# Transpositions of the attention probabilities set between the matmuls of the expert block that follows, in a kernel of block attention and two mixture layers

## The chip, the cores and the metric

One core of a Trainium2 chip runs one program. The metric is device time in microseconds (us), the median of several executions; lower is better. The engines are PE (TensorE, matmuls; PEld is its loading of stationary operands), DVE (VectorE), ACT (ScalarE), POOL (GpSimd) and SP (SyncE, which issues the transfers). Each engine takes its own instructions strictly in the order in which they were recorded, and waits where one of them needs another engine's result.

## What is computed

Three stages follow one another: attention with a mask of 64-wide blocks (4 batches, 8 heads, 576 positions, head width 64), a layer that takes the largest of three products, and a gated layer.

```python
scores = np.where(block_i >= block_j, scale * np.matmul(q, k.transpose(0, 1, 3, 2)), -1e9)
attn = np.exp(scores - np.max(scores, axis=-1, keepdims=True))
attn = attn / (np.sum(attn, axis=-1, keepdims=True) + 1e-09)
x = np.matmul(attn, v)                      # 2304 tokens of 512
h = np.maximum(np.maximum(x @ w1, x @ w2), x @ w3)      # 768 wide
x = h @ w_out
gate = 1.0 / (1.0 + np.exp(-(x @ w_gate)))              # 1536 wide
out = gate * (x @ w_val) @ w_out2
```

## The kernel before

**Jobs.** A job is the attention of one batch and one pair of heads. The 16 early jobs take the first 256 positions, the 16 late jobs the other 320. A late job makes scores for head 0 and head 1 (`scores`, L390 and L391) and for the last 64 positions of both heads (`scores_four`, L460 and L461), takes maxima and exponentials on DVE and ACT, divides by the sums in place (tiles `E0`, `E1` and `E4`), transposes the probabilities on PE (`turn`, L493: 7 transpositions of 128x128 for each head in a late job, 3 in an early one; `turn_four`, L509: 4 and one of 64 columns), copies them out of PSUM into `PT` (`keep`, `keep_four`; lines L81 and L85 are the shared copy helper on ACT and DVE), and multiplies by the values (`apply`, L531). A late job's 7 transpositions fall into a group of 4 and a group of 3, each with a PSUM tile `ps_t` of its own. There are two such tiles, so a third group waits until the first has been copied out.

**Chunks.** The first layer runs in chunks 0 to 7 of 256 or 320 tokens: chunks 0 to 3 are the early halves (256 columns), 4 to 7 the late ones (320 columns). A chunk has 18 expert blocks, named here f0 to f5 with w0, w1 and w2 for the three weights (`experts`, L564 to L566), each of 12 matmuls that fill one tile `ps_m`, and four output blocks (`project`, L630 to L632) of 18. There are two `ps_m` tiles, so each block waits until the tile of the block before the last has been read. Reading it (`larger`) is ACT's copy for w0 and DVE's maximum (L603) for w1 and w2. After w2 the result is split into a high half on ACT (L614) and a low half on DVE (L90, tile `HR`), which the output blocks read. Chunk 0 uses another form (L584 and L592). The second layer (from 488 us) has no attention beside it.

**What runs beside what.** While chunk i runs, four jobs of the next chunk's attention run between its blocks: jobs of early halves in chunks 0 to 2, late jobs in chunks 3 to 6. PE takes both in one stream.

**What sets the order.** The kernel builds a list of operations (`Op`) with estimated costs, plans start times on all engines with them (`plan`), and records everything by planned start (`run_plan`). The chip then runs each engine's recorded order; the estimates set the order alone. `pe(...)` gives the cost of an operation on PE, `lat` and 0.25 us are added behind an operation of PE before its readers may start, and `LEN` spaces out the parts of the jobs. The planned cost of a group of transpositions is 0.109 us each and 0.02.

```python
kp = Op(*both(128 * len(g), True), lambda e, h=h, g=g: keep(j, h, g, e), [o] + pold)
o.frees = [kp]
```

These two lines say that the copy depends on its group of transpositions and that the group's `ps_t` tile is free when the copy is done; `both` lets the plan choose DVE or ACT.

Of the kernel before, what the change touches and what calls it, by code (L numbers as in the profile page):

```python
# [20 lines left out]
KD = DM // 128  # L21
# [12 lines left out]
QKN = 2 * S + 640  # L34

NEAR = 6


PLAN = {
# [27 lines left out]
def block_attention_moe_moe(ctx: ExitStack, tc, k1, q1, v1, k2, q2, vt, wa, wb, out):  # L67
# [3 lines left out]
    P = PLAN  # L71
# [65 lines left out]
    class Op:  # L137
# [3 lines left out]
        def __init__(self, eng, cost, f, deps, pos=None, ring=None, late=None, size=0):  # L141
            self.eng, self.cost, self.f = eng, cost, f
            self.deps = [d for d in deps if d is not None]
            self.pos, self.ring, self.late, self.size = pos, ring, late, size
            self.frees = []
            self.end = None
            self.late_pools = False
            ops.append(self)

    def act(n, acc=0):  # L150
# [8 lines left out]
    def plan():  # L159
# [60 lines left out]
        while left:  # L220
            picks = []
            for e in "PVAS":
                if e == "P":
                    c = choose([s[0] for s in pe if s], e)
                elif e in "VA":
                    c = choose(pools[e] + pools["B"], e)
                    if c is not None and c[1].eng == "B":

                        o, x = c[1], "VA"["AV".index(e)]
                        mine, other = o.cost["VA".index(e)], o.cost["VA".index(x)]  # L230
                        if max(free[x], c[2]) + other + 0.02 < c[2] + mine + (P["lean"] if e == "V" else 0.0):
                            c = choose(pools[e], e) if pools[e] else None
                else:
                    c = choose(pools[e], e)
                if c is not None:
                    picks.append((c[2], e, c[1]))
            assert picks, "the plan is stuck"
            t, e, o = min(picks, key=lambda x: (x[0], "SPVA".index(x[1])))
            cost = o.cost["VA".index(e)] if o.eng == "B" else o.cost
            if e == "P" and t < P["cold"]:  # L240
                cost *= 1.9
            o.start, o.on = t, e
            free[e] = t + cost
            o.end = t + cost
            if e == "S" and o.size:
                wire[0] = max(wire[0], t) + o.size / P["rate"]
                o.end = wire[0]
            if o.ring:
                rings[o.ring].append(o)
            if e == "P":  # L250
                pe["AM".index(o.stream)].pop(0)
            else:
                pools[o.eng].remove(o)
            for s in succ[o]:
                waiting[s] -= 1
                if waiting[s] == 0 and s.eng != "P":
                    pools[s.eng].append(s)
            left -= 1
# [12 lines left out]
    def run_plan():  # L271
        if SHOW:
            for o in sorted(ops, key=lambda o: o.start):
                if o.eng == "P":
                    print(f"{o.start:.2f} {o.end:.2f} {o.stream} {o.ring} pos {o.pos:.2f}")
            for e in "PVAS":
                print(e, sum(o.end - o.start for o in ops if o.on == e), max(o.end for o in ops if o.on == e))
            for w in range(0, 600, 25):
                print(w, [round(sum(max(0, min(o.end, w + 25) - max(o.start, w)) for o in ops if o.on == e), 1) for e in "PVA"])
        spare = []  # L280
        tensor = sorted([o for o in ops if o.eng == "P"], key=lambda o: o.start)
        end = 2.0
        for o in tensor:
            if o.ring == "m":
                break
            n = int((o.start - end) / P["turn"][bool(spare)])
            if n > 0:
                x = Op("P", 0.0, lambda n=n: keep_warm(n), [])
                x.start = end + 0.01
                spare.append(x)  # L290
            end = o.end
        for o in sorted(ops, key=lambda o: o.start):
            if o.late_pools and not WB:
                open_pools()
            at(o.start)
            o.f(o.on) if o.eng == "B" else o.f()

    warm = []

# [181 lines left out]
    def recip_four(j):  # L481
# [3 lines left out]
        )  # L485
        V.reciprocal(j.rc4, j.rc4)

    def turn(j, h, g):

        ps = ps_t.tile([128, 512], F32, tag="t", name="ps_t")  # L490
        for i, (k, t) in enumerate(g):
            e = EO[t] + j.eo + 128 * k
            T.transpose(ps[:, 128 * i : 128 * i + 128], E[h][:, e : e + 128], ident)  # L493
        j.tp[h, g[0]] = ps

    def keep(j, h, g, e):
# [8 lines left out]
    def turn_four(j, i):  # L505
        ps = ps_t.tile([128, 512], F32, tag="t", name="ps_t4")
        for k in ((0, 1, 2, 3), (4,))[i]:
            r = 64 if k == 4 else 128
            T.transpose(ps[0:r, 128 * (k % 4) : 128 * (k % 4) + 128], E4[:, 128 * k : 128 * k + r], ident)  # L509
        j.tp4[i] = ps.rearrange("p (k h c) -> p k h c", k=4, h=2)  # L510

    def keep_four(j, i, e):
# [44 lines left out]
    def experts(i, f, w):  # L557
        c = i // B
        n = CH1[c][1]
        xh, xl = xt(i, c, 0), xt(i, c, 1)  # L560
        ps = pm.tile([128, 512], F32, tag="m", name="ps_m")[:, :n]
        wt = W[f].rearrange("p s (w k c) -> p s w k c", w=3, k=KD)
        for k in range(KD):
            T.matmul(ps, wt[:, 0, w, k], xh[:, k], start=(k == 0), stop=False)  # L564
            T.matmul(ps, wt[:, 0, w, k], xl[:, k], start=False, stop=False)  # L565
            T.matmul(ps, wt[:, 1, w, k], xh[:, k], start=False, stop=(k == KD - 1))  # L566
        pss[i, f, w] = ps


# [50 lines left out]
    def project(i, d, fs):  # L620
        n = CH1[i // B][1]
        if 0 in fs:
            pss[i, d] = pm.tile([128, 512], F32, tag="m", name="ps_m")[:, :n]
        ps = pss[i, d]
        cd = slice(128 * d, 128 * d + 128)
        for f in fs:
            hh, hl = hcols(i, f)
            wo = W[6 + f // 3].rearrange("p s (f c) -> p s f c", f=3)
            wh, wl = wo[:, 0, f % 3, cd], wo[:, 1, f % 3, cd]
            T.matmul(ps, wh, hh, start=(f == 0), stop=False)  # L630
            T.matmul(ps, wh, hl, start=False, stop=False)
            T.matmul(ps, wl, hh, start=False, stop=(f == NF1 - 1))  # L632

    def stage(i, d, e):
        n = CH1[i // B][1]
# [47 lines left out]
    for j in jobs:  # L683
# [4 lines left out]
        else:  # L688
# [3 lines left out]
                v[0] = [(p, "T0"), (p, "T1")] + v[0]  # L692
            visits += v
    visits += [[], [(jobs[-1], "P")]]
    LEN = {"S0": (0, 0.82), "S1": (0.8, 0.82), "S4": (0, 1.06), "T0": (0.35, 0.77),
           "T1": (0.35, 0.77), "T4": (0, 0.5), "P": (0.95, 2.5)}
    place = {}
    ends = []
    for n, v in enumerate(visits):
# [36 lines left out]
    def build():  # L736
# [99 lines left out]
        def job(j):  # L836
# [94 lines left out]
            def turns(h):  # L931
                ns = [
                    Op(*both(128 * (t + 1), False), lambda e, h=h, k=k: norm(j, h, k, e), [rc[h]])
                    for k, t in enumerate(j.tiles)
                ]
                for q, g in enumerate(groups):
                    o = pe("A", 0.109 * len(g) + 0.02, lambda h=h, g=g: turn(j, h, g), ns, pos(f"T{h}") + 0.1 * q, ring="t")
                    kp = Op(*both(128 * len(g), True), lambda e, h=h, g=g: keep(j, h, g, e), [o] + pold)
                    kp.late = pos(f"T{h}") + P["keep"]
                    o.frees = [kp]  # L940
                    j.t_ops[h].append(o)
                    keeps.append(kp)

            def turns_four():
                for q in range(2):
                    o = pe("A", (0.45, 0.06)[q], lambda q=q: turn_four(j, q), [n4], pos("T4") + 0.1 * q, ring="t")
                    ks = [Op(*both((384, 128)[k], True), lambda e, k=k: keep_four(j, k, e), [o] + pold) for k in range(2)] if q == 0 else [
                        Op(*both(128, True), lambda e: keep_four(j, 2, e), [o] + pold)]
                    for k in ks:
                        k.late = pos("T4") + P["keep"]  # L950
                    o.frees = ks
                    j.t_ops[4].append(o)
                    keeps.extend(ks)
# [21 lines left out]
        def chunk(i):  # L975
# [5 lines left out]
            for f in range(NF1):  # L981
                m = []
                for w in range(3):
# [4 lines left out]
                        landed[3 * f + w].frees.append(o)  # L988
                    else:
                        o = pe("M", 12 * CM[c], lambda f=f, w=w: experts(i, f, w), deps, pos, ring="m")  # L990
                    if i == 2 * B - 1:
                        users[f].append(o)
                    if w == 0:
# [18 lines left out]
            for d in range(KD):  # L1012
# [16 lines left out]
                if i == 2 * B - 1:  # L1029
                    users[6].extend(done)  # L1030
                    users[7].extend(done)
                st = Op(*both(n, True), lambda e, d=d: stage(i, d, e), done, ring="st")
                st.late = pos + mcost(i, NF1) + P["evac"]
                o.frees = [st]
# [215 lines left out]
```

## Time and profile before

| | us |
|---|---|
| median of 3 runs (944.55 to 945.87) | 945.73 |
| profiled execution, its own time | 944.49 |
| its span, first to last instruction | 942.7 |
| PE busy | 934.0 (99%) |
| PEld busy | 865.3 (92%) |
| DVE busy | 475.2 (50%) |
| ACT busy | 379.6 (40%) |
| POOL busy | 0.7 |

Matmuls are pipelined: a row's duration is the way of one matmul through the engine, and what a matmul takes from its successors is the distance between their starts. Behind a group of transpositions the first matmul is recorded as started early and lasts longer; the start of the second matmul behind is free of that. PE's granted clock is 1.00 of full speed (the 2.4 GHz level) from 36 us on.

### The profile page before, as it was taken

The numbers are of one execution on the slowest core, as the hardware profiler recorded it, in microseconds if no ns is written. First come the engines' busy times: TensorE is split into PE (matmuls) and PEld (weight loads), VectorE is DVE, ScalarE is ACT, GpSimd is POOL, SyncE is SP. The second block draws the span as 40 slices with busy tenths as digits, with TensorE's granted clock in tenths as the row PEclk, the third lists the DMA queues.
The fourth block names the chain that finished last, engine by engine and source line by source line (L and its number), as shares of the span: only waits on it lengthen the run. The fifth ranks groups of instructions, "written<-read, shape, count | busy, mean of one in ns | idle before, by whom it ended". The sixth has DMA issues, their size and how long they took to land.

```text
span 942.7 us, 14791 instructions
## 1 busy us (share of the span) xinstructions
PE 934.0 (99%) x5891; PEld 865.3 (92%) x5891; DVE 475.2 (50%) x1215; ACT 379.6 (40%) x901; POOL 0.7 (0%) x6
## 2 busy tenths in 40 slices
PE   7999999999999999999999999999999999999998
PEld 6888999999999999999999999999999999999997
DVE  5998546786776776765359961122113112112111
ACT  5946433565654655653247742112112112111111
POOL 0000000000000000000000000000000000000000
PEclk9999999999999999999999999999999999999999
DMA  8921123222122323102047750001000000000000
GB/s 296 363 62 57 35 86 99 64 93 78 54 77 82 121 79 104 40 1 69 27 159 258 263 182 34 1 3 48 1 1 34 1 1 34 1 0 1 34 1 34
DMA packets 38437, 70.16 MB, mean 74 GB/s; under 512 B 5856, under 2 KB 23264, under 8 KB 38368
## 3 DMA queue, kind: packets, MB, share of 16 engines
q1 hardware_dynamic: 38368, 69.22, 22.1%
q8 instruction: 46, 0.75, 0.3%
q14 instruction: 23, 0.19, 0.1%
HBM read 59.77 MB, written 9.44 MB: 73 GB/s over the span
## 4 chain that ended last, share of the span: by engine, by line
PE 98%; SPq 1%; DMA 0%; DVE 0%; issue 0%; ACT 0%
PE ps_m L564 7%; PE ps_m L565 7%; PE ps_m L566 7%; PE ps_g L1145 5%; PE ps_g L1143 5%; PE ps_out L1174 5%; PE ps_out L1175 5%; PE ps_g L1144 5%; PE ps_v L1145 5%; PE ps_v L1143 5%; PE ps_v L1144 5%; PE ps_out L1173 5%; PE ps_o L531 5%; PE ps_t L493 4%; PE ps_m L584 3%; PE ps_m L630 3%
## 5 line engine op out<-in xcount | busy, mean ns | idle before, releaser
L1153 DVE TENSOR_TENSOR gv<-ps_v,sg 128x384 f32<-128x384 f32 x72 | 40.1, 557 | 269.2 <-PE ps_v L1145 253.1
L564 PE MATMUL ps_m<-XT,w 128*128 128x320 f32 (+1 forms) x504 | 155.1, 308 | 0.0
L566 PE MATMUL ps_m<-XT,w 128*128 128x320 f32 (+1 forms) x504 | 150.2, 298 | 0.0
L565 PE MATMUL ps_m<-XT,w 128*128 128x320 f32 (+1 forms) x504 | 150.1, 298 | 0.0
L1149 ACT ACTIVATE sg<-ps_g 128x384 f32<-128x384 f32 x72 | 35.4, 491 | 178.0 <-PE ps_g L1145 178.0
L564 PEld LDWEIGHTS ps_m<-XT,w 128*128 128x128 f32 x504 | 95.4, 189 | 3.4 <-issue 1.9
L565 PEld LDWEIGHTS ps_m<-XT,w 128*128 128x128 f32 x504 | 95.5, 190 | 0.7
L566 PEld LDWEIGHTS ps_m<-XT,w 128*128 128x128 f32 x504 | 95.3, 189 | 0.0
L1160 ACT CAST HR<-gv 128x384 fp32r<-128x384 f32 x72 | 36.9, 512 | 129.1 <-DVE gv L1153 128.9
L439 ACT ACTIVATE E<-ps_s,nm 128x384 f32<-128x384 f32 (+1 forms) x124 | 64.6, 528 | 54.1 <-DVE nm L434 34.5
L603 DVE TENSOR_TENSOR m<-ps_m,m 128x320 f32<-128x320 f32 (+1 forms) x90 | 41.3, 459 | 55.6 <-PE ps_m L566 52.7
L1145 PE MATMUL ps_g<-XT,w 128*128 128x384 f32 x192 | 64.8, 338 | 0.0
L1143 PE MATMUL ps_g<-XT,w 128*128 128x384 f32 x192 | 64.7, 337 | 0.0
L1143 PE MATMUL ps_v<-XT,w 128*128 128x384 f32 x192 | 64.2, 334 | 0.0
L1145 PE MATMUL ps_v<-XT,w 128*128 128x384 f32 x192 | 64.2, 334 | 0.0
L1175 PE MATMUL ps_out<-w,HR 128*128 128x512 f32 x144 | 57.0, 396 | 0.0
L1174 PE MATMUL ps_out<-w,HR 128*128 128x512 f32 x144 | 56.9, 395 | 0.0
L1173 PE MATMUL ps_out<-w,HR 128*128 128x512 f32 x144 | 56.0, 389 | 0.0
L90 DVE TENSOR_TENSOR HR<-gv,HR 128x384 fp32r<-128x384 f32 x72 | 40.2, 558 | 30.6 <-ACT HR L1160 30.6
L434 DVE TENSOR_REDUCE nm<-ps_s 128x1 f32<-128x384 f32 (+1 forms) x124 | 54.0, 470 | 0.8
L531 PE MATMUL ps_o<-PT,v 128*64 128x320 f32 (+3 forms) x448 | 50.5, 365 | 3.3 <-DVE PT L85 3.3
L630 PE MATMUL ps_m<-HR,w 128*128 128x320 f32 (+1 forms) x168 | 51.8, 308 | 0.0
(136 smaller groups left out, 2071.6 us busy)
## 6 DMA issues: line engine op xcount, KB each, us to landing
wraw<-in_wb_dram SPq DMA_DIRECT2D x36, 512.0 KB, 4.5
wland<-in_wa_dram SPq DMA_DIRECT2D x6, 1536.0 KB, 16.7
qk<-in_k_dram SPq DMA_DIRECT2D x16, 576.0 KB, 4.0
v<-in_vt_dram SPq DMA_DIRECT2D x16, 320.0 KB, 2.9
xraw<-x2d SPq DMA_DIRECT2D x12, 384.0 KB, 3.6
out_dram<-osb SPq DMA_DIRECT2D x18, 256.0 KB, 2.1
wraw<-in_wa_dram SPq DMA_DIRECT2D x6, 512.0 KB, 5.7
qk<-in_q_dram SPq DMA_DIRECT2D x16, 160.0 KB, 4.3
```

The source lines that it names most:

```text
L439: A.activation(E[h][:, e : e + 128 * (t + 1)], j.s[h, t], AF.Exp, bias=j.nm[:, c : c + 1], scale=1.0 if j.late else SCALE, accum_out=j.sm[ ...
L531: T.matmul(j.o[rows(h), d : d + n], j.v[:, h, k, :], PT[:, h, c : c + n], start=(k == 0), stop=(k == len(parts) - 1), skip_group_check=True,)
L564: T.matmul(ps, wt[:, 0, w, k], xh[:, k], start=(k == 0), stop=False)
L565: T.matmul(ps, wt[:, 0, w, k], xl[:, k], start=False, stop=False)
L566: T.matmul(ps, wt[:, 1, w, k], xh[:, k], start=False, stop=(k == KD - 1))
L630: T.matmul(ps, wh, hh, start=(f == 0), stop=False)
L1143: T.matmul(ps, w[:, 0, i, k], xh[:, k], start=(k == 0), stop=False)
L1144: T.matmul(ps, w[:, 0, i, k], xl[:, k], start=False, stop=False)
L1145: T.matmul(ps, w[:, 1, i, k], xh[:, k], start=False, stop=(k == KD - 1))
L1173: T.matmul(ps, gh[:, ct], wh, start=(f == 0), stop=False)
L1174: T.matmul(ps, gh[:, ct], wl, start=False, stop=False)
L1175: T.matmul(ps, gl[:, ct], wh, start=False, stop=(f == NF2 - 1))
```

## The change

The transpositions are no longer recorded where their operation stands. `turn` and `turn_four` put them on a list, and the next operation of PE decides: if it is an expert or output block of chunks 1 to 7, `matmul` records the listed transpositions one by one among that block's matmuls, evenly; if it is anything else, or if a copy that reads them is recorded first, they are recorded at once, in a row, as before.

The estimates change too. In late jobs and all but the first few early ones (`i > 3`) a transposition now costs 0.068 us in the plan instead of 0.109, a group counts as done 0.25 us times its number of transpositions later (`lag`), and `LEN` is shorter for the three parts with transpositions.

```diff
+TC = (0.109, 0.068)
+TLAG = 0.25
...
+            self.lag, self.blends = 0.0, False
...
-            o.end = t + cost
+            o.end = t + cost + o.lag
...
+        due = []
         for o in sorted(ops, key=lambda o: o.start):
...
+            if due and (o.eng == "P" and not (o.blends or o.lag) or any(d in due for d in o.deps)):
+                turn_some(len(turns_due))
+                due = []
+            if o.lag:
+                due.append(o)
             at(o.start)
             o.f(o.on) if o.eng == "B" else o.f()
+            if o.eng == "P" and not o.lag:
+                turn_some(len(turns_due))
+                due = []
...
+    def turn_some(n):
+        for _ in range(n):
+            o, x = turns_due.pop(0)
+            T.transpose(o, x, ident)
+
+    def among(n):
+
+        shares[:] = [0, n, len(turns_due)]
+
+    def matmul(*a, **k):
+        i, n, m = shares
+        if turns_due:
+            turn_some(-((-(i + 1) * m) // n) - (m - len(turns_due)))
+        shares[0] += 1
+        T.matmul(*a, **k)
...
-            T.transpose(ps[:, 128 * i : 128 * i + 128], E[h][:, e : e + 128], ident)
+            turns_due.append((ps[:, 128 * i : 128 * i + 128], E[h][:, e : e + 128]))
...
+        among(3 * KD)
...
-            T.matmul(ps, wt[:, 0, w, k], xh[:, k], start=(k == 0), stop=False)
+            matmul(ps, wt[:, 0, w, k], xh[:, k], start=(k == 0), stop=False)
...
-    LEN = {"S0": (0, 0.82), "S1": (0.8, 0.82), "S4": (0, 1.06), "T0": (0.35, 0.77),
-           "T1": (0.35, 0.77), "T4": (0, 0.5), "P": (0.95, 2.5)}
+    LEN = {"S0": (0, 0.82), "S1": (0.8, 0.82), "S4": (0, 1.06), "T0": (0.35, 0.5),
+           "T1": (0.35, 0.5), "T4": (0, 0.36), "P": (0.95, 2.5)}
...
-                    o = pe("A", 0.109 * len(g) + 0.02, lambda h=h, g=g: turn(j, h, g), ns, pos(f"T{h}") + 0.1 * q, ring="t")
+                    o = pe("A", TC[i > 3] * len(g) + 0.02, lambda h=h, g=g: turn(j, h, g), ns, pos(f"T{h}") + 0.1 * q, ring="t")
+                    if i > 3:
+                        o.lag = TLAG * len(g)
...
-                    o = pe("A", (0.45, 0.06)[q], lambda q=q: turn_four(j, q), [n4], pos("T4") + 0.1 * q, ring="t")
+                    o = pe("A", (4, 1)[q] * TC[1] + 0.02, lambda q=q: turn_four(j, q), [n4], pos("T4") + 0.1 * q, ring="t")
+                    o.lag = TLAG * (4, 1)[q]
```

The place shown below is the second job of chunk 5 (about 324 to 332 us in the trace of before). On PE before, its 7 transpositions of `E0` stand in a row between block f2 w0 (`ps_m_3955`) and block f2 w1 (`ps_m_3987`):

```order
L566 MATMUL ps_m_3955<-XT_76,w_848 128x320
L493 MATMUL ps_t_3977<-ident_101,E0_107 128x128 x4
L493 MATMUL ps_t_3983<-ident_101,E0_107 128x128 x3
L564 MATMUL ps_m_3987<-XT_76,w_848 128x320
L565 MATMUL ps_m_3987<-XT_76,w_848 128x320
```

On PE now, from the third transposition of `E0` in that job on; the block around them, `ps_m_3990`, is f2 w2, `ps_m_4017` is f3 w0 and `ps_m_4045` is f3 w1:

```order
L512 MATMUL ps_t_3985<-ident_101,E0_107 128x128
L523 MATMUL ps_m_3990<-XT_76,w_847 128x320 x2
L512 MATMUL ps_t_3985<-ident_101,E0_107 128x128
L523 MATMUL ps_m_3990<-XT_76,w_847 128x320
L512 MATMUL ps_t_3987<-ident_101,E0_107 128x128
L523 MATMUL ps_m_3990<-XT_76,w_847 128x320 x2
L512 MATMUL ps_t_3987<-ident_101,E0_107 128x128
L523 MATMUL ps_m_3990<-XT_76,w_847 128x320 x2
L512 MATMUL ps_t_3987<-ident_101,E0_107 128x128
L523 MATMUL ps_m_3990<-XT_76,w_847 128x320 x2
L523 MATMUL ps_m_4017<-XT_76,w_909 128x320 x12
L512 MATMUL ps_t4_4032<-ident_101,E4_109 128x128
```

The last transposition of `E0` now stands behind ten of the block's twelve matmuls, and the row of seven became seven rows of one.

On DVE before, the same job: the two copies of `E0`'s transpositions, the low half `L` of the next job's keys, two small operations on the sums, the maximum that reads `ps_m_3987`, and what follows:

```order
L377 SCALAR_TENSOR_TENSOR Q1_104<-qk_3810,Q1_104 64x320 x2
L85 COPY PT_110<-ps_t_3977 128x4x128
L85 COPY PT_110<-ps_t_3983 128x3x128
L90 TENSOR_TENSOR L_106<-qk_3582,K_105 128x1152
L447 TENSOR_SCALAR rc_3885<-sm_3884 128x2
L448 RECIPROCAL rc_3885<-rc_3885 128x2
L603 TENSOR_TENSOR m1_4032<-ps_m_3987,m0_4003 128x320
L87 TENSOR_SCALAR E1_108<-E1_108,rc_3885 128x384
L85 COPY PT_110<-ps_t4_4006 128x2x64
L85 COPY PT_110<-ps_t4_4011 64x2x64
L603 TENSOR_TENSOR m2_4043<-ps_m_4013,m1_4032 128x320
```

On DVE now, the same job:

```order
L89 COPY PT_110<-ps_t_3987 128x3x128
L89 COPY PT_110<-ps_t_3985 128x4x128
L94 TENSOR_TENSOR L_106<-qk_3571,K_105 128x1152
L463 TENSOR_SCALAR rc_3899<-sm_3898 128x2
L464 RECIPROCAL rc_3899<-rc_3899 128x2
L641 TENSOR_TENSOR m2_4041<-ps_m_3990,m1_3954 128x320
L91 TENSOR_SCALAR E1_108<-E1_108,rc_3899 128x384
L89 COPY PT_110<-ps_t4_4038 64x2x64
L393 SCALAR_TENSOR_TENSOR Q1_104<-qk_3811,Q1_104 64x320 x2
L89 COPY PT_110<-ps_t4_4032 128x2x64
L94 TENSOR_TENSOR HR_1025<-m2_4041,HR_1025 128x320
L641 TENSOR_TENSOR m1_4072<-ps_m_4045,m0_4039 128x320
```

The copy of the later group (`ps_t_3987`, three transpositions) moved ahead of that of the earlier one, the maximum behind the chain is now that of the block that holds the transpositions (`ps_m_3990`), and the products for `Q1` moved between the two copies of `E4`'s transpositions.

## Rows read from the trace of the kernel before

**Rows 1.** The page: span, PE's busy time, and the chain that ended last.

```profile
span 942.7 us, 14791 instructions
PE 934.0 (99%) x5891; PEld 865.3 (92%) x5891; DVE 475.2 (50%) x1215; ACT 379.6 (40%) x901; POOL 0.7 (0%) x6
PE 98%; SPq 1%; DMA 0%; DVE 0%; issue 0%; ACT 0%
```

**Rows 2.** All waits of PE: who waited for whom, us, times, longest.

```profile
PE ps_o L531 <- DVE PT L85: 3.3, 1, 3.3
PE ps_w L306 <- POOL ident masks.py:199: 1.4, 1, 1.4
PE ps_s L411 <- DMA qkv<-in_q_dram: 0.4, 1, 0.4
```

**Rows 3.** Timeline of PE: start, us, line; one transposition alone among matmuls of 256.

```profile
207.96 0.28 PE L565 MATMUL ps_m<-XT,w 128*128 128x256 f32 x1
208.08 0.28 PE L566 MATMUL ps_m<-XT,w 128*128 128x256 f32 x1
208.20 0.27 PE L509 MATMUL ps_t<-ident,E 128*64 128x128 f32 x1
208.23 0.36 PE L564 MATMUL ps_m<-XT,w 128*128 128x256 f32 x1
208.43 0.28 PE L565 MATMUL ps_m<-XT,w 128*128 128x256 f32 x1
```

**Rows 4.** Timeline of PE: seven transpositions in a row among matmuls of 320.

```profile
346.52 0.31 PE L565 MATMUL ps_m<-XT,w 128*128 128x320 f32 x1
346.67 0.31 PE L566 MATMUL ps_m<-XT,w 128*128 128x320 f32 x1
346.82 0.93 PE L493 MATMUL ps_t<-ident,E 128*128 128x128 f32 x7
347.50 0.40 PE L564 MATMUL ps_m<-XT,w 128*128 128x320 f32 x1
347.73 0.30 PE L565 MATMUL ps_m<-XT,w 128*128 128x320 f32 x1
```

**Rows 5.** Timeline of DVE, second job of chunk 5: start, us, line, idle before.

```profile
324.58 1.08 DVE L434 TENSOR_REDUCE nm<-ps_s 128x1 f32<-128x384 f32 x2
325.69 0.89 DVE L377 SCALAR_TENSOR_TENSOR Q<-qk,Q 64x320 fp32r<-64x320 f32 x2
326.67 1.16 DVE L85 COPY PT<-ps_t 128x512 f32<-128x512 f32 x2
327.74 1.35 DVE L90 TENSOR_TENSOR L<-qk,K 128x1152 fp32r<-128x1152 f32 x1
329.00 0.16 DVE L447 TENSOR_SCALAR rc<-sm 128x2 f32<-128x2 f32 x1
329.20 0.17 DVE L448 RECIPROCAL rc<-rc 128x2 f32<-128x2 f32 x1
329.29 0.49 DVE L603 TENSOR_TENSOR m<-ps_m,m 128x320 f32<-128x320 f32 x1
329.69 0.41 DVE L87 TENSOR_SCALAR E<-E,rc 128x384 f32<-128x384 f32 x1
330.02 0.47 DVE L85 COPY PT<-ps_t 128x128 f32<-128x128 f32 x2
331.82 0.56 DVE L85 COPY PT<-ps_t 128x384 f32<-128x384 f32 x1 [0.27 <-PE ps_t L493]
```

**Rows 6.** Timeline of PE, the same job: its transpositions and the next block.

```profile
326.03 0.93 PE L493 MATMUL ps_t<-ident,E 128*128 128x128 f32 x7
330.86 0.93 PE L493 MATMUL ps_t<-ident,E 128*128 128x128 f32 x7
331.54 0.40 PE L564 MATMUL ps_m<-XT,w 128*128 128x320 f32 x1
```

**Rows 7.** Groups by line (busy us, mean ns, idle before): low halves of h, DVE.

```profile
L90 DVE TENSOR_TENSOR HR<-m,HR 128x320 fp32r<-128x320 f32 (+1 forms) x42 | 19.2, 458 | 8.0 <-ACT HR L614 7.6
```

**Rows 8.** Busy us by engine in two stretches: chunks 1 to 3, chunks 4 to 6.

```profile
core 0: us, PE busy (x) PEld busy (x) DVE busy (x) ACT busy (x) POOL busy (x), PEclk, DMA share, GB/s
84.00:236.00 152.00, 152.00 (x1246) 140.68 (x1245) 100.83 (x299) 73.15 (x208) 0.00 (x0) 1.00 0.24 73
236.00:437.00 201.00, 201.00 (x1444) 187.46 (x1443) 141.36 (x378) 116.61 (x283) 0.00 (x0) 1.00 0.21 66
```

More of the change, by code (lines that the diff above doesn't have):

```diff
@@ L486, in recip_four @@
         V.reciprocal(j.rc4, j.rc4)
+    turns_due = []
+    shares = [0, 0, 0]
+    def turn_some(n):
[10 more added lines that the diff above has]
+        T.matmul(*a, **k)
     def turn(j, h, g):
@@ L508, in turn_four @@
             r = 64 if k == 4 else 128
-            T.transpose(ps[0:r, 128 * (k % 4) : 128 * (k % 4) + 128], E4[:, 128 * k : 128 * k + r], ident)
+            turns_due.append((ps[0:r, 128 * (k % 4) : 128 * (k % 4) + 128], E4[:, 128 * k : 128 * k + r]))
         j.tp4[i] = ps.rearrange("p (k h c) -> p k h c", k=4, h=2)
@@ L562, in experts @@
         wt = W[f].rearrange("p s (w k c) -> p s w k c", w=3, k=KD)
+        among(3 * KD)
         for k in range(KD):
-            T.matmul(ps, wt[:, 0, w, k], xh[:, k], start=(k == 0), stop=False)
-            T.matmul(ps, wt[:, 0, w, k], xl[:, k], start=False, stop=False)
-            T.matmul(ps, wt[:, 1, w, k], xh[:, k], start=False, stop=(k == KD - 1))
+            matmul(ps, wt[:, 0, w, k], xh[:, k], start=(k == 0), stop=False)
+            matmul(ps, wt[:, 0, w, k], xl[:, k], start=False, stop=False)
+            matmul(ps, wt[:, 1, w, k], xh[:, k], start=False, stop=(k == KD - 1))
         pss[i, f, w] = ps
@@ L625, in project @@
         cd = slice(128 * d, 128 * d + 128)
+        among(3 * len(fs))
         for f in fs:
@@ L629, in project @@
             wh, wl = wo[:, 0, f % 3, cd], wo[:, 1, f % 3, cd]
-            T.matmul(ps, wh, hh, start=(f == 0), stop=False)
-            T.matmul(ps, wh, hl, start=False, stop=False)
-            T.matmul(ps, wl, hh, start=False, stop=(f == NF1 - 1))
+            matmul(ps, wh, hh, start=(f == 0), stop=False)
+            matmul(ps, wh, hl, start=False, stop=False)
+            matmul(ps, wl, hh, start=False, stop=(f == NF1 - 1))
     def stage(i, d, e):
@@ L990, in chunk @@
                         o = pe("M", 12 * CM[c], lambda f=f, w=w: experts(i, f, w), deps, pos, ring="m")
+                        o.blends = True
                     if i == 2 * B - 1:
@@ L1031, in chunk @@
                     users[7].extend(done)
+                for o1 in done:
+                    o1.blends = i > 0
                 st = Op(*both(n, True), lambda e, d=d: stage(i, d, e), done, ring="st")
```

## The prediction

> **What bounds the kernel now.** I read the chain that ended last first: 98% of the span is PE [rows 1]. Then PE's waits: three in the whole run, 5.1 us together, all in the first 19 us [rows 2]. From chunk 1 on PE is busy in every stretch (152.00 of 152, 201.00 of 201 us), with DVE at 66% and 70% and a granted clock of 1.00 [rows 8]. So from chunk 1 on the time is the sum of what PE's instructions take from one another. A change can gain only by making one of them cheaper, and every wait that it puts on PE is paid in full. Two questions decide: what a transposition costs between two matmuls, and whether the copies behind the transpositions still come in time.
>
> **What a spread transposition costs.** Seven in a row: from the first start to the start of the second matmul behind them 347.73 - 346.82 = 0.91 us, less that matmul's predecessor's own 0.147 (346.67 to 346.82) leaves 0.763, or 0.109 each [rows 4]. The trace of before also holds the form that the change makes: one transposition alone between two expert blocks. There 208.43 - 208.20 = 0.23, less the 0.12 that a matmul of 256 columns takes (207.96 to 208.08), leaves 0.11 [rows 3]. So alone costs as much as in a row. That row loads 64 columns of probabilities where most have 128, but it streams the same 128 columns and a load is under way while the matmul ahead runs; a larger load gives no reason for a lower price. The change spreads 234 of the 400 transpositions (222 alone, 6 pairs); the rest are in chunk 0's time, or, like the 7 of `E1` in 15 of 16 late jobs, still stand in a row, since what follows them there is no expert block. At 0.11 against 0.109 the spreading is worth 0 to -0.3 us. Lower bound of the price: half of a 256-column matmul, 0.06, which would give 234 x 0.049 = 11.5 us back. I take 0.11, since the row is the thing itself.
>
> The Trainium skill, "TensorE: Matmul & The Clock Gate", speaks for that lower bound: section "Back-to-back issue gap" gives 128 / 2.4 + 2.5 = 56 ns for 128 columns, and "Weight-path perf modes" says that a load of 128 columns of a type other than FP32 is fast, so the matmul behind would not be held up. By it the gain would be an estimated 234 x 0.053 = 12.4 us. The single row at 0.11 disagrees.
>
> **What the copies cost now.** The planned lag is 1.0 us behind a group of four and 0.75 behind a group of three, so the plan expects the later group of three first and puts its copy first. On the chip the transpositions are spread through the whole block, and the last comes late. I set 0 at the first transposition of `E0` and walk the second job of chunk 5. The last one starts behind ten matmuls and six transpositions: 10 x 0.147 + 6 x 0.109 = 2.12. It ends 0.27 later, and a copy starts 0.03 behind the end of its group (330.86 + 0.93 = 331.79, copy at 331.82 [rows 5, 6]): 2.42. DVE, which takes its instructions in order, stands at that copy. Its reductions of the scores run as in before from 0.4 to 1.5, so it is free by then. Behind the two copies stand the low half of the keys, the two small operations and the maximum that frees the block's `ps_m`; the same chain in before took 329.29 + 0.49 - 326.67 = 3.11 [rows 5]. So `ps_m` comes free at 5.53. PE reaches the block that needs it (f3 w1, two blocks on) at 12 x 0.147 + 7 x 0.109 = 2.53, plus 1.76 for f3 w0, plus 0.11 for one transposition of `E4`: 4.40. With 0.05 for the hop, an estimate from the 0.03 above, PE waits **1.2 us**. In before the chain began at 326.67 and its `ps_m` was wanted at 331.54 behind the `E1` row [rows 6], 1.76 us after 329.78: covered. That cover is gone.
>
> The same job waits again. PE resumes at 5.58; nine matmuls and three transpositions on, the last of `E4` starts at 7.23 and ends at 7.50. DVE copies it at 7.53, then takes the two `Q1` products (0.89) and then the second copy (the two copies 0.47 [rows 5]): 8.89. The seven transpositions of `E1` need that `ps_t`; PE is there after three matmuls, at 7.23 + 0.11 + 0.44 = 7.78: **1.15 us**. Chunks 4 and 6 have the same order in this job.
>
> Fourth job of chunks 4 to 6: copies (1.07 to the next start) and maximum (0.40) from 2.42, then the low half of the keys (1.26) and only then the low half of h of f5 (0.46 [rows 7]): 5.61. The output block's second matmul on f5 wants it at 2.53 + 15 x 0.147 + 4 x 0.109 + 0.147 = 5.32: **0.35 us**. First and third job: the maximum is ahead of the long operation, or ACT reads the block; no wait by the same walk. Sum for a chunk 2.7, for three **8.1 us**.
>
> Chunk 3 has 256 columns (0.12 each), and its last transposition is copied at 10 x 0.12 + 0.65 + 0.30 = 2.15. Second job: chain to the reciprocal's end 2.62, then a copy of `E4`'s last transposition (0.23) and a normalisation (0.33) ahead of the maximum (0.42): 5.75 against 2.20 + 1.44 + 5 x 0.11 = 4.19, **1.6**. Third job: DVE stands at the copy of `E4`'s last transposition, which starts at 3.64 + 9 x 0.12 + 4 x 0.109 = 5.16 and ends at 5.43, then 0.23 + 0.33 + 0.42 to the `ps_m` that f5 w0 wants at 5.63: 6.44, **0.85**. Fourth: low half of h at 5.25 against 4.67, **0.6**. Together **3.05 us**. Chunks 1 and 2 have early jobs, whose copies are followed by short operations, and two blocks or more of cover; 0.
>
> **The rest.** PE records the same instructions in the same number; DVE takes 27 more and ACT 27 fewer, some 0.5 us each of copies and scalings, over 353 us in which DVE is busy 242 [rows 8]: no bound of its own, but part of why both copies stand on DVE. The stage from 488 us is untouched in order. The last job's `E1` is spread three matmuls ahead of `apply`: 0 to 0.3.
>
> **The sum.** 8.1 + 3.05 + 0.2 = 11.3 us, against the profiled execution's own 944.49 (span 942.7 and 1.8 around it): 955.8. The median of the three runs lies 1.2 above that execution: 945.73 + 11.3 = **957.0**. Thirteen waits make the sum. If each link is 0.4 us quicker than in the walk, 11.3 - 5 gives 952; if each is 0.4 slower, 962.
>
> **The rivals.** *The transposition is cheap among matmuls.* For it: the columns themselves, 0.06. Against it: the single row, and the first transposition of each row, whose load was covered by a matmul and which still takes 0.109. Alone it gives 945.7 - 11.5 = 934; together with the waits 945.7 - 11.5 + 11.3 = 945.5, no change. *The copies hold nobody up* (not slower): PE gives DVE time elsewhere, or the copy of three does not stand at the last transposition, because its group ended sooner. The place is DVE's chain behind that copy, the price 1.2 us a job, and the point is a chain that ends before 4.40; it would have to be 1.1 us shorter than the 3.11 measured. Then the time is 945.7 to 946. For it: no wait at all in before, so the plan leaves room. Against it: the room of that chain was 1.76 and the block's spreading takes 1.36 of transposition time (2.12 - 0.76) on top of an order in which the wanted tile is one block earlier. *The change doesn't spread*: 166 of 400 are unspread, the others are in the recorded order, so this is out.
>
> **Chances.** Waits of 6 to 16 us: 0.72 (951.5 to 962). Smaller waits, 2 to 6 us: 0.06. Above 962: 0.04. Hardly any wait: 0.11. Cheap with waits: 0.04; cheap without: 0.03. About 0.2% (1.9 us) is what a measurement of this kernel can tell from no change, so faster 0.04, same 0.14, slower 0.82. The range holds the likeliest case and reaches down to the case without waits: 946 to 962.
>
> **What would show it.** Right: PE's waits on DVE's maximum (`m`) and on `PT` appear in the second job of chunks 3 to 6, 1 us or more each, and on `HR` in the fourth; the single transpositions are 0.11 apart from their matmul; DVE stands idle ahead of the copy of the group of three until the last transposition's end, about 2.4 us behind the first one. Wrong: the matmul behind a spread transposition starts 0.06 to 0.07 after it, or chunks 4 to 6 end as early as before.

## The result

954.81 us (median; 953.65 to 955.26) against 945.80 for the kernel before in the same runs: a ratio of 1.0091, 95% interval 1.0076 to 1.0106. The change makes the kernel 9.0 us slower. The prediction was 957.0, with a range of 946.0 to 962.0 and 0.82 on slower.

The page of the changed kernel: span, and busy time of each engine with the number of instructions (compare [rows 1]).

```profile
span 952.9 us, 14788 instructions
PE 939.0 (99%) x5891; PEld 864.8 (91%) x5891; DVE 484.5 (51%) x1242; ACT 366.5 (38%) x874; POOL 0.7 (0%) x6
```

PE's instructions are as many as before, DVE has 27 more and ACT 27 fewer. The waits of PE tell more. In before it had none after 19 us [rows 2]; now, from 84 to 500 us (who waited for whom, us in total, times, longest us):

```profile
PE ps_t L512 <- DVE PT L89: 1.8, 3, 0.6
PE ps_m L523 <- ACT m L639: 1.2, 3, 0.4
PE ps_m L523 <- DVE HR L94: 1.2, 4, 0.5
PE ps_m L523 <- DVE m L641: 0.7, 1, 0.7
```

Eleven waits, 4.9 us. A wait also costs what lies around it (matmuls that were in flight count as busy, and PE starts again slowly), so the whole price is better read from the lengths of the chunks: from the start of a chunk's first matmul to that of the next chunk's. The first matmul of chunk 5 starts at 305.73 in before, that of chunk 6 at 376.61; now it is 311.26 and 384.36:

```profile
305.73 0.31 PE L564 MATMUL ps_m<-XT,w 128*128 128x320 f32 x1
...
376.61 0.31 PE L564 MATMUL ps_m<-XT,w 128*128 128x320 f32 x1
```

```profile
311.26 0.46 PE L523 MATMUL ps_m<-XT,w 128*128 128x320 f32 x2
...
384.36 0.46 PE L523 MATMUL ps_m<-XT,w 128*128 128x320 f32 x2
```

So 70.88 us became 73.10. Worked out in the same way for every chunk (chunk 7 up to the first matmul of the second layer), from starts in ns:

| chunk | before, us | changed kernel, difference |
|---|---|---|
| 1 | 45.41 | -0.03 |
| 2 | 45.03 | -0.01 |
| 3 | 63.02 | +2.31 |
| 4 | 70.88 | +2.22 |
| 5 | 70.88 | +2.22 |
| 6 | 69.01 | +2.22 |
| 7 | 42.24 | 0.00 |

Together +8.9, which is the whole of the 9.0. The start of chunk 1 moves by up to 2.4 us from one profiled execution to another (81.4 in before, 82.4 here, 83.8 in one of the experiments) and is taken for noise: the executions of the kernel before alone lie from 943.79 to 947.46 us beside the first experiments. The chunks repeat to a few hundredths, and the experiments are read from them.

**Where the three losses of a chunk lie.** Chunk 5's second job on PE (start, us, engine, line, operation, shape, count, and in brackets the idle time ahead and what ended it), with the first and the last transposition of `E0` at its head:

```profile
333.32 0.27 PE L512 MATMUL ps_t<-ident,E 128*128 128x128 f32 x1
...
335.46 0.27 PE L512 MATMUL ps_t<-ident,E 128*128 128x128 f32 x1
335.49 2.29 PE L523 MATMUL ps_m<-XT,w 128*128 128x320 f32 x14
337.62 0.27 PE L512 MATMUL ps_t<-ident,E 128*128 128x128 f32 x1
338.29 0.56 PE L523 MATMUL ps_m<-XT,w 128*128 128x320 f32 x2 [0.41 <-ACT m L639]
...
340.70 0.66 PE L512 MATMUL ps_t<-ident,E 128*128 128x128 f32 x4
341.94 0.55 PE L512 MATMUL ps_t<-ident,E 128*128 128x128 f32 x3 [0.59 <-DVE PT L89]
```

The first loss is ahead of block f3 w1: a matmul behind a transposition is recorded 0.03 after it, here 0.68 after it. That is 0.65 later, and with the slower restart (0.25 to the next start instead of 0.23) about 0.68 in all. The second is in the row of `E1`, whose starts should be 0.109 apart: the fifth comes 1.24 after the first instead of 0.44; with 0.10 ahead of the first and 0.06 behind the fifth that is 0.96. The third is in the fourth job, at the output block:

```profile
370.28 0.38 PE L512 MATMUL ps_t<-ident,E 128*128 128x128 f32 x2
370.89 0.41 PE L523 MATMUL ps_m<-HR,w 128*128 128x320 f32 x1 [0.23 <-DVE HR L94]
```

0.61 from the pair's start where 0.11 and 0.03 are usual: 0.47, and with the slower restart about 0.5. 0.68 + 0.96 + 0.50 = 2.14 of the 2.22.

DVE in the second job, the rows that answer to [rows 5]:

```profile
333.63 1.08 DVE L450 TENSOR_REDUCE nm<-ps_s 128x1 f32<-128x384 f32 x2
335.77 1.15 DVE L89 COPY PT<-ps_t 128x384 f32<-128x384 f32 x2 [1.06 <-PE ps_t L512]
336.84 1.35 DVE L94 TENSOR_TENSOR L<-qk,K 128x1152 fp32r<-128x1152 f32 x1
338.11 0.16 DVE L463 TENSOR_SCALAR rc<-sm 128x2 f32<-128x2 f32 x1
338.30 0.17 DVE L464 RECIPROCAL rc<-rc 128x2 f32<-128x2 f32 x1
338.38 0.47 DVE L641 TENSOR_TENSOR m<-ps_m,m 128x320 f32<-128x320 f32 x1
338.77 0.41 DVE L91 TENSOR_SCALAR E<-E,rc 128x384 f32<-128x384 f32 x1
340.36 0.28 DVE L89 COPY PT<-ps_t 64x128 f32<-64x128 f32 x1 [1.19 <-PE ps_t L512]
340.68 0.89 DVE L393 SCALAR_TENSOR_TENSOR Q<-qk,Q 64x320 fp32r<-64x320 f32 x2
341.60 0.29 DVE L89 COPY PT<-ps_t 128x128 f32<-128x128 f32 x1
```

It is done with the reductions at 334.71 and stands idle for 1.06 at the copy of the group of three, as forecast; they start 335.77 - 333.32 = 2.45 us behind the first transposition (2.42 forecast). Then L, reciprocal and the maximum, to 338.85. From 84 to 437 us DVE's waits for a `ps_t` ahead of a copy grew from 6.9 to 24.8 us. In before the transpositions have two lines, L493 for `E0` and `E1` and L509 for `E4`; now all have one. The rows of before and of now:

```profile
DVE PT L85 <- PE ps_t L493: 6.7, 15, 0.9
DVE PT L85 <- PE ps_t L509: 0.2, 1, 0.2
```

```profile
DVE PT L89 <- PE ps_t L512: 24.8, 30, 1.2
```

One thing in these rows is not as forecast. The maximum that should have freed the tile for f3 w1 starts at 338.38, and PE goes on at 338.29, ahead of it. What ended its wait is ACT's copy of f3 w0, of the block that had only just ended; it ends at 338.24, 0.05 ahead of PE's start:

```profile
337.82 0.43 ACT L639 COPY m<-ps_m 128x320 f32<-128x320 f32 x1 [1.54 <-PE ps_m L523]
```

### The profile page after: what moved, and what is told of

It is laid out like the page before. It is cut to its first block, busy times and chain, and to the rows that moved or that the text cites. A ratio compares the mean times of both kernels' runs of the same rounds, so it can differ in the third digit from the quotient of the medians.

```text
span 952.9 us, 14788 instructions
## 1 busy us (share of the span) xinstructions
PE 939.0 (99%) x5891; PEld 864.8 (91%) x5891; DVE 484.5 (51%) x1242; ACT 366.5 (38%) x874; POOL 0.7 (0%) x6
## 4 chain that ended last, share of the span: by engine, by line
PE 96%; DVE 2%; SPq 1%; DMA 1%; issue 0%; ACT 0%
PE ps_m L523 28%; PE ps_g L1190 5%; PE ps_g L1188 5%; PE ps_out L1219 5%; PE ps_g L1189 5%; PE ps_out L1220 5%; PE ps_v L1190 5%; PE ps_v L1188 5%; PE ps_v L1189 5%; PE ps_out L1218 5%; PE ps_o L568 5%; PE ps_t L512 4%; PE ps_m L622 3%; PE ps_s L406 2%; PE ps_s L407 1%; PE ps_s L427 1%
## 5 line engine op out<-in xcount | busy, mean ns | idle before, releaser
L523 PE MATMUL ps_m<-XT,w 128*128 128x320 f32 (+1 forms) x1512 | 236.3, 310 | 1.9 <-ACT m L639 1.2
L523 PEld LDWEIGHTS ps_m<-XT,w 128*128 128x128 f32 x1512 | 212.6, 189 | 8.3 <-ACT m L639 2.2
L512 PE MATMUL ps_t<-ident,E 128*128 128x128 f32 (+1 forms) x400 | 86.3, 275 | 1.8 <-DVE PT L89 1.8
L523 PE MATMUL ps_m<-HR,w 128*128 128x320 f32 (+1 forms) x504 | 75.4, 303 | 1.2 <-DVE HR L94 1.2
L523 PEld LDWEIGHTS ps_m<-HR,w 128*128 128x128 f32 x504 | 69.7, 189 | 3.2 <-DVE HR L94 2.1
L89 DVE COPY PT<-ps_t 128x384 f32<-128x384 f32 (+3 forms) x89 | 45.9, 531 | 31.1 <-PE ps_t L512 29.4
L512 PEld LDWEIGHTS ps_t<-ident,E 128*128 128x128 f32 (+1 forms) x400 | 51.7, 140 | 4.7 <-DVE PT L89 3.3
```

What stands on the lines that cost most here:

```text
L89: n.tensor_copy(out, in_)
L512: T.transpose(o, x, ident)
L523: T.matmul(*a, **k)
```

## The experiments

Differences are those of chunks 3 to 6 against the kernel before, from starts of matmuls as above; chunks 1, 2 and 7 stay within 0.05 us in all of them.

| run | chunk 3 | 4 | 5 | 6 | median, us | ratio, 95% interval |
|---|---|---|---|---|---|---|
| changed kernel | 2.31 | 2.22 | 2.22 | 2.22 | 954.81 | 1.0091 (1.0076 to 1.0106) |
| row_in_new_plan | 0.23 | 0.23 | 0.23 | 0.23 | 947.05 | 1.0010 (1.0000 to 1.0020) |
| spread_over_6 | 0.83 | 1.01 | 1.02 | 1.04 | 950.31 | 1.0043 (1.0026 to 1.0060) |
| spread_over_9 | 1.41 | 1.77 | 1.76 | 1.75 | 952.28 | 1.0065 (1.0045 to 1.0085) |
| four_first | 1.50 | 1.73 | 1.73 | 1.69 | 953.32 | 1.0071 (1.0052 to 1.0089) |
| tiles_alternate | 3.35 | 2.80 | 2.81 | 2.84 | 956.57 | 1.0113 (1.0098 to 1.0128) |
| row_tiles_alternate | 1.35 | 0.00 | 0.00 | 0.00 | 947.01 | 1.0013 (1.0003 to 1.0022) |
| three_on_ACT | 1.69 | -0.45 | 2.44 | -0.74 | 948.86 | 1.0025 (1.0015 to 1.0036) |
| late_lag_alternate | 2.23 | 1.57 | 1.55 | 1.59 | 953.32 | 1.0078 (1.0061 to 1.0095) |
| e4_copy_on_ACT | 2.33 | 1.37 | 1.38 | 1.38 | 951.86 | 1.0060 (1.0043 to 1.0077) |

### In a row, in the new plan

```diff
             turns_due.append((ps[:, 128 * i : 128 * i + 128], E[h][:, e : e + 128]))
+        turn_some(len(turns_due))
         j.tp[h, g[0]] = ps
```

(and the same line in `turn_four`.)

> The changed kernel with its plan (costs, lags, the order of every engine) as it is, but each group of transpositions recorded at once, in a row, where its operation stands. Theory A (the waits come from the last transposition coming 2.4 us after the first, with DVE's in-order copies behind it): the seven end 0.93 us after the first, 1.5 us earlier than when spread; the waits of the second job of chunks 4 to 6 (0.68 and 0.95) and of the fourth (0.5) are gone, and those of chunk 3; time 945.8 to 947, chunks 3 to 6 within 0.5 us of the kernel before. Theory B (the waits come from the plan's new order: group of three first, Q1 between the copies of E4, 27 more operations on DVE, however early the transpositions come): they stay, 952 to 955. Theory C (a transposition among matmuls costs more or less than one in a row): the time of the row moves by 234 x the difference; at the 0.108 read from the changed kernel's trace that is nothing.

947.05, and 0.23 a chunk is left of 2.2. The second and the third loss of the result are gone, and of the first 0.23 is left; the order on DVE is the changed kernel's own. So what costs is how late the last transposition comes, and not the new order alone. Where that 0.23 comes from is shown below.

### Spread over nine and over six matmuls

The edit for six; for nine it has 9 in the place of 6.

```diff
-            turn_some(-((-(i + 1) * m) // n) - (m - len(turns_due)))
+            turn_some(min(m, -((-(i + 1) * m) // 6)) - (m - len(turns_due)))
```

> The changed kernel with the transpositions spread over the first nine of a block's matmuls instead of all twelve. Theory A: the last of E0's seven stands behind 7 matmuls instead of 10, 0.44 us earlier, so the first wait of the second job falls from 0.68 to about 0.25; the last of E4's five behind 7 instead of 9, 0.29 earlier, so the second falls from 0.95 to about 0.65; the fourth job's 0.5 to about 0.1. Per chunk 1.0 instead of 2.2, chunk 3 about 1.2 instead of 2.3; time about 950 (949 to 951.5). Theory B: 954 to 955, unchanged.

> The same over the first six matmuls. Theory A: the last of E0's seven behind 5 matmuls and two more of them in pairs, 0.73 us earlier than over twelve: the first wait 0, the second 0.95 - 0.73 = 0.2, the fourth job's 0; chunk 3 about 0.5; time 946 to 948. Theory B: 954 to 955.

Less spreading, less loss, in order: 12 matmuls 2.22, 9 1.76, 6 1.02, a row 0.23. That is the sign of theory A, but both runs came out slower than it said (1.0 and about 0.2 a chunk). The trace names the remainder. Over six, in chunk 5's second job, the fourth job's loss is 0 and that of `E1` about 0.23 (its fifth start is 0.28 behind the fourth instead of 0.11, and the next 0.165), but the first is what it was: the matmul behind the first transposition of `E4` comes 0.677 after it (0.678 over twelve). A chain that starts 0.73 earlier behind the first transposition did not move it. DVE's maximum there starts at 336.47 and ends at 336.94; PE goes on at 337.11, again behind ACT's copy:

```profile
333.86 1.16 DVE L89 COPY PT<-ps_t 128x384 f32<-128x384 f32 x2 [0.34 <-PE ps_t L512]
...
336.47 0.47 DVE L641 TENSOR_TENSOR m<-ps_m,m 128x320 f32<-128x320 f32 x1
```

```profile
336.44 0.27 PE L512 MATMUL ps_t<-ident,E 128*128 128x128 f32 x1
337.11 0.42 PE L523 MATMUL ps_m<-XT,w 128*128 128x320 f32 x1 [0.41 <-ACT m L639]
```

### The four copied first

```diff
                     if i > 3:
-                        o.lag = TLAG * len(g)
+                        o.lag = TLAG * (4 if j.late else len(g))
```

> The changed kernel with the lag of the later group of three set to that of the group of four (1.0 us), which moves the copy of the four ahead of the copy of the three on DVE and changes nothing else in the late jobs. Theory A: the four end about 1.3 us before the last transposition, so their copy (0.56) is done while DVE would have stood still, and the chain behind the last one is 0.56 shorter: first wait of the second job 0.68 to about 0.1, the fourth job's 0.5 to 0, the second wait (E4's copies with Q1 between them) stays 0.95; chunk 3 about 1 us less; time 954.8 - 3 x 1.05 - 1 = 950.6 (949.5 to 952). Theory B holds that the order alone costs: then this wins only where the order is part of it, and the time is the same figure; the two are told apart by the other runs of this call.

953.32 instead of 950.6. As expected the fourth job's loss is gone and that of `E1` stays, and chunk 3 lost 0.8. The first stays at 0.678: again it does not follow DVE's chain.

### The two tiles strictly in turn

The rows of the changed kernel said that f3 w1 waits for ACT's copy of f3 w0. The program shows why: with its two `ps_m` buffers the pool hands a new block the one whose reader was recorded first. The new plan expects DVE's maximum of f2 w2, behind the copies and L, later than ACT's copy of f3 w0, so that copy is recorded first, and f3 w1 gets the buffer of the block just ahead of it. This is so at four blocks of 176 in the changed kernel (the second job of chunks 3 to 6) and at none in before. That a block waits for the tile of the block before the last, as the text ahead of the prediction has it, is so for every block of before, and not for these four. The experiment takes the buffers in turn:

```diff
-    pm = ctx.enter_context(tc.tile_pool(name="pm", bufs=RING["m"], space=PSUM))
+    pms = [ctx.enter_context(tc.tile_pool(name=f"pm{i}", bufs=1, space=PSUM)) for i in range(2)]
+    class pm:
+        n = 0
+        def tile(*a, **k):
+            pm.n += 1
+            return pms[pm.n % 2].tile(*a, **k)
```

> The changed kernel with the two ps_m tiles taken strictly in turn. In the changed kernel the pool gives a block the tile whose reader was recorded first, and in the second job of chunks 3 to 6 that is the tile of the block just before (f3 w0, read by ACT) instead of that of the block before the last (f2 w2, read by DVE's maximum): its first wait (0.68) ends with ACT's copy at 338.24, not with DVE's maximum at 338.85. Theory A1 (the chain on DVE behind the last transposition is as the prediction walked it, and only the tile was another): with the tiles in turn the block waits for the maximum, 0.6 us longer in that job of chunks 3 to 6: chunks 4 to 6 at 2.8 above the kernel before instead of 2.2, chunk 3 at 2.9; time 954.8 + 2.4 = 957.2. Theory A2 (the first wait is nothing but the choice of the tile): with the tiles in turn it is gone, chunks 4 to 6 at 1.5 to 1.6, time 952.3.

956.57, with chunks 4 to 6 at 2.80 to 2.84: theory A1. (Chunk 3 lost more than expected, 3.35 where 2.9 was; the next run shows the place.) The matmul now waits for DVE's maximum, as the prediction had walked it. PE and DVE of that run, chunk 5's second job:

```profile
339.25 0.27 PE L520 MATMUL ps_t<-ident,E 128*128 128x128 f32 x1
340.55 0.56 PE L531 MATMUL ps_m<-XT,w 128*128 128x320 f32 x2 [1.02 <-DVE m L649]
```

```profile
337.40 1.16 DVE L89 COPY PT<-ps_t 128x384 f32<-128x384 f32 x2 [1.06 <-PE ps_t L520]
...
340.02 0.47 DVE L649 TENSOR_TENSOR m<-ps_m,m 128x320 f32<-128x320 f32 x1
```

The maximum ends at 340.49, PE goes on at 340.55: 1.30 from the transposition instead of 0.03, a wait of 1.27 where the prediction had 1.2. The changed kernel's pool gives f3 w1 the tile of the block just ahead of it and comes off better for it: it waits for a copy of 0.43 instead.

> The run with the transpositions in a row in the new plan, with the two ps_m tiles taken in turn. That run stood 0.23 us a chunk above the kernel before in chunks 3 to 6; if this is ACT's copy of the tile of the block just before, which a row of five transpositions (0.55) covers but for that, then with the tiles in turn the chunks 1 to 7 are as long as in the kernel before (each within 0.05 us) and the time is 945.8 to 946.3. If the new order on DVE costs anything by itself, 0.2 us a chunk or more is left.

With the transpositions in a row and the buffers in turn, chunks 4 to 6 are as long as in before to 0.01 us: the 0.23 was ACT's copy. This is the cleanest reading of the plan without the spreading: there its order costs nothing. Chunk 3 is a miss, 1.35, and the time with it (947.01 where 945.8 to 946.3 was expected). There one block waits 1.03 for DVE's maximum, behind a row of five transpositions of `E4`:

```profile
196.89 0.71 PE L520 MATMUL ps_t<-ident,E 128*128 128x128 f32 x5
198.64 0.62 PE L531 MATMUL ps_m<-XT,w 128*128 128x256 f32 x3 [1.03 <-DVE m L651]
```

So in the shorter blocks of chunk 3 the new order on DVE does cost something even in a row, which the free choice of the buffer had hidden.

### Copies put on ACT

The group of three in the late jobs:

```diff
-                    kp = Op(*both(128 * len(g), True), lambda e, h=h, g=g: keep(j, h, g, e), [o] + pold)
+                    late3 = j.late and len(g) == 3
+                    kp = Op(*(act(384) if late3 else both(128 * len(g), True)), lambda e="A", h=h, g=g: keep(j, h, g, e), [o] + pold)
```

> The changed kernel with the late jobs' copies of groups of three put on ACT; the plan then orders the rest anew. Spreading is as in the changed kernel (232 alone). Theory A (DVE stands at the copy behind the last transposition, and what is queued behind it comes late): DVE's copy of the four is ready 1.1 us sooner, the chain behind it ends at about 3.7 of the 4.4 us; waits of the second and fourth jobs are gone, chunks 3 to 6 within 0.4 us of the kernel before (one block still takes the tile of the block before it), time 946 to 947.5. Theory B (DVE's work as such is too much, or PE runs worse with transpositions among the matmuls): 1 us a chunk or more is left, 950 and above.

948.86: with 232 transpositions alone among matmuls the loss falls from 8.9 to 2.9 us, which speaks for theory A, but the expected 946 to 947.5 is missed. The plan shifts work between chunks 4 to 6, so only their sum with chunk 3 counts. Half of what is left is a new wait that I had not costed: twice the scores of the last 64 positions wait for an exponential on ACT, 0.71 each from start to start. The copies on ACT are not what holds it up. ACT stands idle 0.65 ahead of that exponential, for DVE's row maxima of scores that PE had only just made; and the new plan has two sets of these scores directly behind one another, where in the changed kernel other matmuls stand between them (the sets start at 375.62 and 378.79 there, at 376.59 and 377.83 here). Another 0.68 is the one block, an output block of chunk 5, that still gets the buffer of the block ahead of it.

```profile
PE ps_s L476 <- ACT E L455: 1.1, 2, 0.6
PE ps_m L523 <- ACT x2s L85: 0.4, 1, 0.4
```

```profile
377.11 0.58 ACT L455 ACTIVATE E<-ps_s,nm 128x384 f32<-128x384 f32 x1 [0.65 <-DVE nm L450]
```

The 128x128 copy of `E4`'s first group alone:

```diff
-                    ks = [Op(*both((384, 128)[k], True), lambda e, k=k: keep_four(j, k, e), [o] + pold) for k in range(2)] if q == 0 else [
+                    ks = [Op(*(act(128) if k else both(384, True)), lambda e="A", k=k: keep_four(j, k, e), [o] + pold) for k in range(2)] if q == 0 else [
```

> The changed kernel with one copy moved: the 128x128 copy of the first group of E4's transpositions is ACT's instead of DVE's. On DVE the order of the late jobs is otherwise the same, with the two products for Q1 in their place. Theory A (the second wait of the second job, 0.96 in chunks 4 to 6, is this copy standing behind the two products, 0.89): ACT takes it about 340.0 and the seven transpositions of E1 find their tile free: the wait is gone, chunks 4 to 6 at 1.26 above the kernel before instead of 2.22, chunk 3 about 0.2 to 0.3 less than 2.31; the first wait (0.68) and the fourth job's (0.5) stay; time 954.8 - 3.1 = 951.7. Rival (the tile is held by another copy, or ACT's queue makes the copy just as late): the wait stays, 954 to 955.

951.86, as expected (951.7). Chunks 4 to 6 fall by 0.85 (0.96 expected), and the row of `E1` runs through, its seven transpositions in 0.98 (0.93 in before [rows 6]):

```profile
341.04 0.98 PE L512 MATMUL ps_t<-ident,E 128*128 128x128 f32 x7
```

So the second loss is that copy standing behind the two products for `Q1`, but for about 0.12 that stays. Chunk 3 did not move (2.33), against the 0.2 to 0.3 that I had expected there: in its second job the changed kernel has that copy ahead of the products already (198.36 and 198.68).

### A lag nearer to the chip

```diff
-TC = (0.109, 0.068)
+TC = (0.109, 0.109)
...
-                        o.lag = TLAG * len(g)
+                        o.lag = (1.0, 1.6)[q] if j.late and h == 0 else 1.0
...
-                    o.lag = TLAG * (4, 1)[q]
+                    o.lag = (1.2, 1.6)[q]
```

(with the tiles in turn.)

> The changed kernel with a plan that knows more of the chip: 0.109 us for every transposition, a lag of 1.0 for the group of four and 1.6 for the group of three of E0 (1.2 and 1.6 for E4's two), so that the four are copied first and the products for Q1 stand ahead of the copies, and with the ps_m tiles in turn. 228 transpositions are alone among matmuls. Theory A: the second wait of the second job (0.96, by Q1 between the copies of E4) is gone, the fourth job's too; the chain behind the last transposition is the copy of the three, the keys' low half, reciprocal and maximum, to 5.0 against 4.4: 0.6 us a job left, chunks 4 to 6 about 0.6 above the kernel before, time about 948.5 (947 to 950). That spreading saves something by itself: chunks 1 to 6 below the kernel before, which theory A excludes at 0.108 us each.

953.32, a miss by 5. The order came out as wanted, with the four first and `Q1` ahead of both copies, but the products (0.89) now keep DVE busy until the copies can both go, so the chain behind them starts hardly earlier:

```profile
334.18 0.89 DVE L401 SCALAR_TENSOR_TENSOR Q<-qk,Q 64x320 fp32r<-64x320 f32 x2
335.10 1.16 DVE L89 COPY PT<-ps_t 128x512 f32<-128x512 f32 x2
336.17 1.35 DVE L94 TENSOR_TENSOR L<-qk,K 128x1152 fp32r<-128x1152 f32 x1
```

The first wait is 1.15 of the 1.57. My expectation had taken the copy of the four out of the chain, though nothing in the order had it ready before the last transposition ended.

### The price of a transposition

```diff
         for _ in range(n):
             o, x = turns_due.pop(0)
+            if x.shape[1] == 128:
+                shares.append(0)
+                if len(shares) % 2:
+                    T.transpose(o[0:64], x[:, 0:64], ident)
+                else:
+                    T.transpose(o[:, 0:64], x[0:64], ident[0:64, 0:64])
             T.transpose(o, x, ident)
...
-        i, n, m = shares
+        i, n, m = shares[:3]
```

> The changed kernel with a second, narrower transposition recorded ahead of most 128x128 ones, which overwrites it; the result is the same and the time is longer for it. Two kinds take turns: one with 64 columns of probabilities as the loaded operand and 128 moving columns, one with 64 rows, so 128 loaded columns and 64 moving ones. Read from the trace: starts of the pair and of the second matmul behind it. Theory S (the price is the passing of the 128 moving columns): the first kind adds 0.109, the second about half, 0.055 to 0.07. Theory L (the price is the load of the next operand, which the short passing doesn't cover, so that spreading can't help): both add about 0.11, or the first less where its own load is shorter.

PE, among matmuls of 256 columns (0.12 each):

```profile
91.83 0.52 PE L529 MATMUL ps_m<-XT,w 128*128 128x256 f32 x3
92.28 0.27 PE L517 MATMUL ps_t<-ident,E 64*128 64x64 f32 x1
92.49 0.33 PE L518 MATMUL ps_t<-ident,E 128*128 128x128 f32 x1
92.57 0.48 PE L529 MATMUL ps_m<-XT,w 128*128 128x256 f32 x2
92.89 0.27 PE L515 MATMUL ps_t<-ident,E 128*64 128x128 f32 x1
93.00 0.27 PE L518 MATMUL ps_t<-ident,E 128*128 128x128 f32 x1
93.03 0.48 PE L529 MATMUL ps_m<-XT,w 128*128 128x256 f32 x2
```

The first kind (at 92.89, loaded 128*64) adds 0.11: the second matmul behind the pair starts at 93.23 in ns, 0.34 after 92.89, less 0.12 for the matmul makes 0.22 for two. The second kind (at 92.28) does not answer the question: the third matmul ahead of it starts at 91.83 + 0.24 = 92.07, so it comes 0.21 behind that instead of 0.12, and its successor another 0.20 later. From 92.07 to the second matmul behind the pair (92.77 in ns) are 0.70; less two matmuls (0.24) and the full transposition (0.11) that is 0.35, more than either theory had. It has fewer rows and fewer columns at once, so what its 64 columns alone cost can't be read from it. Whether the 0.109 is the columns or the load is left open (the run as a whole took 1035.8 us with its extra transpositions). What the run shows is that 0.11 is paid for 64 loaded columns as for 128.

## Why the prediction was right

**The price of a transposition** was right. In the changed kernel a spread transposition and two matmuls of 256 columns take 0.35, so 0.11 for the transposition, as the single row of before said [rows 3]:

```profile
130.69 0.27 PE L512 MATMUL ps_t<-ident,E 128*128 128x128 f32 x1
130.72 0.48 PE L523 MATMUL ps_m<-XT,w 128*128 128x256 f32 x2
131.04 0.27 PE L512 MATMUL ps_t<-ident,E 128*128 128x128 f32 x1
```

Chunks 1 and 2 are the measurement without any wait: 45 transpositions stand alone there, and the two chunks together are 0.04 us shorter. The rival with the cheap transposition would have taken 45 x 0.049 = 2.2 off. The plan's 0.068 is not what the chip does here.

The Trainium skill, "TensorE: Matmul & The Clock Gate", section "Back-to-back issue gap", has 56 ns for an isolated matmul of 128 columns and about 81 ns in a stream of loads and matmuls. Both are below the 0.11 that a spread transposition takes in this trace where it waits for nothing.

**The late copies** were right. DVE stands 1.06 at the copy of the group of three, and taking the spreading away (row_in_new_plan) takes 8.0 of the 8.9 us away. The rival that the copies hold nobody up is out; the range alone would not have told, since it reaches down to 946, the time of that rival.

**The first wait of the second job, 1.2:** right as a chain, wrong as to what f3 w1 waits for. The chain ends where it was said to end (1.27 with the tiles in turn), but the step "PE reaches the block that needs it (f3 w1)" took for granted that two tiles alternate. They are given by the recorded order of their readers, and f3 w1 gets another: 0.68. The recorded order was there to be read before the run.

**The second wait, 1.15:** 0.96, from the cause named (e4_copy_on_ACT). **The fourth job, 0.35:** 0.50. The sum for a chunk was 2.7 and is 2.22, with the first wait 0.5 too high, the two others 0.04 too high in sum, and 0.08 that the three don't hold.

**Chunk 3, 3.05:** 2.31. The third job's wait is 0.84 (0.85 forecast) and the fourth's 0.65 (0.6), each without 0.1 for the slower restart behind it; the second job's is about 0.4 where 1.6 was forecast, for the same reason, and the remaining 0.4 is these two restarts and two short delays that I did not forecast. (The 2.62 that the walk of chunk 3 calls the reciprocal's end is the start of the maximum behind it, 329.29 - 326.67; that is the figure the walk needs.) **Chunks 1, 2 and 7** were 0 as forecast.

The sum of 11.3 was 8.9. What lies between them is the tile: with the tiles in turn, as the forecast had them, chunks 3 to 6 lose 11.8, against 11.15 forecast for them.

## What to carry to other kernels

When one engine is busy without a gap, moving its instructions among each other gains only if one of them gets cheaper there; find a place in the old trace where the new form already stands, and read its price from that. Spreading a producer delays its last result, and behind an in-order consumer that waits for it everything queued comes later by the same time: walk that queue to the next buffer that the busy engine needs. And where a pool hands out buffers, read from the recorded order which one a block really gets: it can change with the order of the readers, for better or worse.

## What was not expected of the hardware

A transposition with 64 rows among matmuls with 128 costs 0.35 us instead of 0.11, in spite of its 64 columns: it starts 0.21 behind the matmul ahead of it instead of 0.12, and the next 128-row transposition 0.20 behind it. After a wait, PE's next start is further away than usual (0.25 for 0.23, 0.165 for 0.109, 0.22 for 0.12). That is the smaller part of why a wait that the page puts at 0.41 costs 0.68: the page counts the idle time from the end of the transposition's row, 0.27 behind its start, where the next matmul usually starts 0.03 behind it.
